# Adding half of the residual in the output: copies placed early, accumulating transfers from POOL, and a new order of the program

## The chip, the cores and the metric

The kernel runs on one core of a Trainium2 chip. The metric is the device time of one execution in microseconds (us), taken as the median of repeated runs; lower is better. The core has five engines with queues of their own: PE (matrix products into PSUM), DVE and ACT (elementwise work), POOL, and SP, which here issues transfers. ACT and POOL can issue transfers too.

## The reference

The input `x` has 2048 tokens of 512 channels. What is computed (helpers as usual, the convolution by FFT in the reference):

```python
xn = layernorm(x)
# A: a long convolution per channel, its kernel from 128 complex states
K  = einsum("dn,dnl,dn->dl", C, exp(dt * A * l), dt * B).real
s  = causal_conv(xn, K) + xn * Dskip
# B: token shift, then an MLP
h  = gelu(layernorm(xn) @ w1)
x1 = xn + concat(shift(h[0], +1), shift(h[1], -1), shift(h[2], +2), shift(h[3], -2)) @ w2
m  = x1 + gelu(layernorm(x1) @ w3) @ w4
return x + s * silu(m)
```

The last line is the one that the change touches: the gated product `s * silu(m)` is added to the residual `x`.

## The kernel before

The tokens lie in SBUF as `X`, 128 partitions by 16 steps by 512 channels (float32). One tile `X` goes through everything: layernorm, the token shift, the MLP's result, the gate, and at last the product.

The program is a list of some 1600 operations that a recorder (`Plan`) collects with their dependencies. A table of numbers, `ORDER`, says in which order they are issued; a letter behind a number (`a` or `v`) says that ACT or DVE takes an operation that either may do. Each engine runs its own operations strictly in that order, and each queue of transfers is issued in it too: an entry that waits holds up what stands behind it. All operations are issued from one helper line, so the profile's rows all name L310, and they are told apart by tiles.

The stages, much interleaved by the order:

- first layernorm, first product (`hT`), token mixing (tiles `x`, `x2h`, `xT`, `w1h`, `ue`, accumulators `pa` and `pb`);
- sixteen chunks of tables for the convolution's kernel (tiles `wv`, `mag`, `eg`, `up`, `EB`, on ACT and DVE), each ending in small products on PE (`pc`, `kev`, `k1e`);
- the MLP in eight groups of 256 tokens, six steps each: `pb` gets `x1T` times `w3h`, ACT and DVE make `ghl` of it, and `pa` sums `ghl` times `w4h`; a group ends with `X<-pa,wsc,X` on DVE. `x1n`, `x1h` and a transposing transfer prepare a group's input;
- the convolution in the frequency domain, in two halves of 256 channels (`hf` 0 and 1), eight steps each (`uin`, `kin`, `kh`, `pr`, `z1e`), whose results go to DRAM (`scr_Zda`, `scr_Zdb`);
- the gate, `X = silu(X)` on ACT, for each of the eight groups of two steps of tokens;
- the end: for each half and group a load `zin` of the result, a product with `is2` into PSUM (`pd` or `pc` in turn, two pairs of banks), and a multiplication into `X` on DVE (`inverse`). After some groups `finish` adds the residual and stores.

The two functions at the end are these (`V` is DVE, `Q` SP, `A` ACT, `T` PE):

```python
    def inverse(hf, g):
        ...
        Q.dma_start(zin, Zd[hf][:, 2 * g : 2 * g + 2].rearrange("p s r d -> p (s r) d"))
        ...
        V.tensor_mul(Xh, Xh, two[k][:, :, :DH])

    def finish(hf, s0, s1):
        ch = slice(hf * DH, hf * DH + DH)
        xr = resid[hf, s0 // 4]
        V.tensor_add(X[:, s0:s1, ch], X[:, s0:s1, ch], xr[:, s0 % 4 : s0 % 4 + s1 - s0])
        by_r(X[:, s0:s1, ch], ov[:, :, s0:s1, ch], store=(Q, A))
```

`X` no longer holds the residual by then, so `keep_tokens` copies the input from DRAM to DRAM (`scr_Rd`, sixteen transfers of 256 KB at any time in the middle of the program), and `residual` loads it back in eight tiles `xr` of 512 KB ahead of `finish`. The copy's only purpose is a layout that loads in long rows. `by_r` stores the two halves of the partitions, one from SP and one from ACT. The second half (`hf` 1) ends with five calls of `finish`, over 4, 4, 4, 2 and 2 steps of tokens.

The order of the groups in the end is 2, 3, 4, 5, 6, 7, 1, 0; group 0 is the last that the MLP makes.

Of the kernel before, what the change touches and what calls it, by code (L numbers as in the profile page):

```python
# [10 lines left out]
F32 = mybir.dt.float32  # L11
# [3 lines left out]
ALU = mybir.AluOpType  # L15
# [4 lines left out]
P = 128  # L20
L = 2048
D = 512
NM = 128
F = 1376
S = 16
# [90 lines left out]
281 188 71a 138v 204 201 358 63 137 356 279 151 282 276 193 152 197a 222 227 157 283 277 228 229 189 65 284 191 64 285
286 519 192 58 149 206 139 148 359 194a 199 230 231 287 66 198 13 288 195 196 232 212 68 207 205 67 520 521 213v 233
236v 360 365 216a 218 69 529 530 76 250 217 156 254a 215 214 251a 237v 289 361 202 74 75a 256 522 290 255 293a 234v
253 524 525 238v 209 31 239 531 235v 77v 252 134 523 260v 269 273a 270a 241v 242 363 210 211 294v 275 272 526 154 532
533 271 307 153 247 534 535 248 208 244 274 243 291v 308a 311a 245 541 135 292v 326 249 240 366 246 261 528 309 310  # L120
537 312 313 330a 160 161 158 538 536 263 266 29 552 553 327v 328 329 339 295v 296 364 159 155 340a 33 554 257v 258 362
539 558 30 379 555 556 264 371 267 259 540 542 543 561 557 559 32 413 414 415 367 268 368 369 544 545 370 262 572 573
12 298a 299 265 578 372 574 34 304 305 331 332 343a 373 560 427 306 301 546a 374 314a 375 376 377 378 391 35 317a 302
547 562 380 381 563 392 393 428 382 418 297 394 318 416 383 344 395 396 384 300 323 342 397 575 548 385 429 315 576
581 324 386 417 577 579 549a 564 565 303 320 321 432 319 398 592 593 399 566a 580 387 567 400 402 550a 341 388 390 401
594 389 316 325 322 598 336 337 333 334 407 404 338 353 352 410 411a 412 433 408a 409 354 335 347 348 583 551 345 430
711 568 569a 405 582 601 349 346 434 420 421 584 570a 437 585 595 597 422 441 709 596 599 435a 438a 439 458 718 612
403 571 586a 436 425 620 600 459a 625 440 442 621 445 613 622 587 443 452 423 460 602 350 446 426 623 624 461 465 614
603 631 419 424 481 444 431 617 447 448 615 449 616 588 589a 590a 450 511a 515a 618 634 619 464 466 451 482a 604 605
626 453 627 478 483 591 606a 645 516a 485 607 472 517 608 351 462a 484 646 512a 513 647 628 463 712 629 630 632 471  # L130
648 650 514 486 649 609a 518 728 721 722 633 491 636 635 479a 723 651 724a 637 480 494 638 473 735 729 654 492a 610a
611 725 493 500 665 666 726 730 731a 639a 732 742a 743a 736 737 640 495a 497 498a 667 668 744 652 727 738a 499 653 750
751 752 739 733 734 715 655 757 758 753a 641 656 746a 747a 748 745 759 642a 496 764 765 657 658 643a 713 674 671 754
501a 670 685 686 687 740 741 755 756 716 853 659a 669 672 749 770 777 778 766a 760a 761 688 689 762 690 771 772 673
763 773a 660 675 661 767 791a 502 676 406 768 691 706 774 779 780a 784 785 769 775 776 644 662a 692 799 819 714 663a
694 820 821 677 693 792a 793 678 786 664 806 800 822 827 828 807 781 823 782 787a 829 824 825 795a 788 796v 852 469
783 679a 797 798 680 681 456 830 831 682a 695 789 790 826 696 697 698 801 813 802a 794 808 1117 467 683a 832 833 699a
809a 454 684 834 803 814 866 700 838 476 804 835 836 805 810 867 841 837 815a 1124 1118 868 477 1119 468 1125 1126 839
811 816 812 1120a 840 455 701 869 702a 703a 704 817 1131 1132 710 1127a 871 842 843 1121 872 886 818 854 844 845 1146
846a 1138a 1139a 870 1122 900 1123 847 848 901 1140 1141 1133 875 1147 849a 850a 1128 1129 1142a 873 855 1130 1134a  # L140
856a 857 888 902 1135 1143a 874 858 1136 1137 1153 1144 1145 851 719 859 1148 1160 860 861 903 905 904 862 1154 863a
877 1155 876 909 864a 906 865 474 878 879 887 1156a 934 880a 881 1166 935 470 936 1149a 1150 707 882 883a 884a 885
# [12 lines left out]
1267a 1261 489 1048 1070 1064 1103 1090 1065 1066a 1262 1067a 1 1072 1268 1272 1073a 1564 1074 1263 1269 1105 1273
1091 1293 1274a 1075 1076 1285a 1077 1078 1294 1079 1080a 1093 1270 1081a 490 1068 1280 1082 1281a 1094 1095 1096
1097a 1275 1276 1404 1286v 1287 1098 1099 1300 1100a 1101a 1104 1295 1106 1107a 1102 1277 1282 1283 1296v 1289a 1108
1288 1297 1109 1111 1110 1301 1284 1403 1405 1112 1290a 1291 1298 1113 1302 1303v 1114v 487 488 1307 507 1292 1406
1407a 1115v 1308 1419 1408 1409 1410 1411 1299 1313 1431 1418 1314 1315 1412 1413 1415a 1327 1417 1414v 1420 1433 1304
1432 1422 1320 1321 1305 1421a 1423 1424 1425 1426 1427 1322 1309v 1328 1445 508 1517 509 1310 1428a 1434 1435a 1429v  # L160
1436 1116 1306 1316a 1565 510 1311 1334v 1437 1342 1438 1447 1439 1440 1441 1343 1525 1416 1317 1442a 1448 1443v 1449a
1518 1446 1450 1312 1329 1323v 1318 1319 1330a 1324 1325 1451 1452 1453 1454 1455 1456a 1461 1457a 1460 1326 1335v
1336 1344 1331 1338a 1459 1462 1463a 1515 1464 1332 1339v 1340 1349 1465 1475 1466 1467 1350 1468 1345a 1536 1469 1526
1473 1356 1430 1470a 1471v 1337 1351 1476 1474 1357 1478 1333 1341 1369 1488 1362 1477a 1479 1480 1481 1482 1483 1487
1363 1364 1444 1484v 1472 1489 1490 1491a 1501 1346 1485v 1492 1352v 1347 1353 1493 1494 1348 1495 1496 1529 1503 1354
1497 1458 1499v 1519 1355 1498a 1504 1505a 1358v 1359 1520 1502 1506 1566 1360 1507 1370 1524 1500 1376 1508 1567 1371
1509 1510 1511 1513a 1486 1365v 1366 1512v 1383 1514 1527 1521 1539 1372v 1373 1530 1528 1537 1377 1361 1367 1368 1531
# [8 lines left out]
class Plan:  # L176
    def __init__(self, nc):
        self.engines = {"PE": nc.tensor, "ACT": nc.scalar, "DVE": nc.vector, "SP": nc.sync}
# [1119 lines left out]
```

## Time and profile before

| what | value |
|---|---|
| median of 3 runs | 513.03 us (512.98 to 513.2) |
| the profiled execution | 512.22 us, its span 510.3 us |
| PE | 488.5 us busy, 96% of the span |
| DVE | 452.9 us busy, 89% |
| ACT | 397.5 us busy, 78%, of it 65.4 us in 51 loads of function tables |
| POOL | 0.7 us busy |
| transfers | 94.26 MB, 185 GB/s over the span |
| granted PE clock | 0.99 |

Busy shares are averages over stages. A busy PE here includes time in which matrix products wait, so the chain of waits and the rows of the timeline say more than the 96%. In a row of the timeline stand the start, the duration, the engine, the operation, and what it writes and reads; brackets give idle time of the engine before it and what ended that.

### The profile page before, as it was taken

How to read it: one execution, taken by the hardware profiler on the slowest of the kernel's cores; microseconds unless marked ns; L12 is line 12 of the kernel's file. 1: busy time of each engine (PE TensorE's matmuls, PEld its weight loads, DVE VectorE, ACT ScalarE, POOL GpSimd, SP SyncE). 2: the span in 40 equal slices, each digit the busy share in tenths (PEclk: the TensorE clock that was granted, in tenths of full speed). 3: DMA queues.
4: the chain of work that ended last, by engine and by line, in shares of the span. 5: the costliest groups of instructions: out<-in, count | busy, mean ns of one | idle time of the engine just before them, and what ended most of it. 6: DMA issues, size and time to landing. Idle time of an engine off the chain costs nothing.

```text
span 510.3 us, 14368 instructions
## 1 busy us (share of the span) xinstructions
PE 488.5 (96%) x6209; PEld 313.1 (61%) x6209; DVE 452.9 (89%) x633; ACT 397.5 (78%) x591; POOL 0.7 (0%) x6
## 2 busy tenths in 40 slices
PE   8788799999999999999999999999999999999993
PEld 8565376585455866767576656656665665756641
DVE  5899999999999999999999999999994687677376
ACT  3999999979969789999999999997864447254330
POOL 0000000000000000000000000000000000000000
PEclk9899999999999999999999999999999999999998
DMA  8997989699253682350768563694579996977987
GB/s 210 237 248 214 278 248 257 180 211 220 75 111 84 135 166 44 64 83 12 155 147 188 144 181 93 146 146 110 145 204 193 282 383 164 306 251 256 317 291 207
DMA packets 157584, 94.26 MB, mean 185 GB/s; under 512 B 98448, under 2 KB 147856, under 8 KB 157136
## 3 DMA queue, kind: packets, MB, share of 16 engines
q1 hardware_dynamic: 155168, 90.98, 69.8%
q10 hardware_dynamic: 2352, 2.36, 1.6%
q8 instruction: 49, 0.80, 0.7%
q14 instruction: 15, 0.12, 0.1%
HBM read 57.14 MB, written 33.55 MB: 178 GB/s over the span
## 4 chain that ended last, share of the span: by engine, by line
PE 61%; DVE 24%; ACT 10%; issue 3%; DMA 1%; POOLq 0%; SPq 0%; POOL 0%; ACTq 0%; DVEq 0%
PE pb L310 23%; PE pa L310 21%; PE pc L310 11%; DVE wv L310 10%; PE pd L310 6%; DVE X L310 3%; ACT wv L310 3%; DVE ghl L310 2%; ACT wst L310 2%; ACT mag L310 1%; DVE up L310 1%; DVE eg L310 1%; ACT ue L310 1%; DVE stats L310 1%; DMA scr_Ud<-ue 1%
## 5 line engine op out<-in xcount | busy, mean ns | idle before, releaser
L310 PE MATMUL pb<-x1T,w3h 128*128 128x256 f16 (+1 forms) x1056 | 125.1, 273 | 0.3 <-issue 0.3
L310 PE MATMUL pa<-w4h,ghl 128*128 128x512 f16 (+1 forms) x528 | 122.5, 380 | 0.0
L310 PEld LDWEIGHTS <-w3h 128*128 128x128 f16 (+1 forms) x1056 | 101.7, 100 | 27.0 <-issue 10.7
L310 PEld LDWEIGHTS <-ghl 128*128 128x128 f16 (+1 forms) x528 | 48.9, 98 | 62.0 <-issue 10.2
L310 ACT ACT_TABLE_LOAD x51 | 65.4, 1283 | 8.9 <-issue 3.7
L310 ACT ACTIVATE wv<-wv 128x2080 f32<-128x2080 int32 x32 | 62.8, 1963 | 0.5 <-DVE wv L310 0.3
L310 ACT ACTIVATE g<-pb,wsc 128x512 f32<-128x512 f32 (+1 forms) x48 | 30.8, 650 | 22.9 <-PE pb L310 18.3
L310 DVE TENSOR_TENSOR wv<-wv,eg 128x2048 f32<-128x2048 f32 x16 | 36.5, 2283 | 1.6 <-ACT wv L310 1.5
L310 DVE TENSOR_TENSOR wv<-mag,wv 128x2048 f32<-128x2048 f32 x16 | 36.5, 2283 | 0.0
L310 DVE SCALAR_TENSOR_TENSOR ghl<-g,wsc,ghl 128x512 f16<-128x512 f32 (+1 forms) x48 | 33.6, 701 | 2.8 <-ACT ghl L310 2.5
L310 PEld LDWEIGHTS pc<-wv 128*32 128x32 f32 x2048 | 29.8, 109 | 6.1 <-issue 3.4
L310 ACT ACTIVATE wv<-wv,halfpi 128x2080 f32<-128x2080 f32 x16 | 32.9, 2055 | 0.1
L310 ACT ACTIVATE mag<-par 128x128 f32<-128x128 f32 x132 | 32.6, 462 | 0.0
L310 PE MATMUL pc<-wv 128*32 128x64 f32 x2048 | 32.4, 220 | 0.0
L310 ACT ACTIVATE ghl<-g,wsc 128x512 f16<-128x512 f32 (+1 forms) x37 | 25.5, 693 | 8.0 <-PE pa L310 7.2
L310 DVE TENSOR_TENSOR pr<-pd,kh 128x1024 f32<-128x1024 f32 x16 | 19.6, 1223 | 13.0 <-ACT kh L310 11.3
L310 PE MATMUL pb<-xT,w1h 128*128 128x256 f16 x240 | 27.6, 273 | 0.0
L310 PE MATMUL pb<-w,hT 128*128 128x512 f32 x58 | 26.6, 599 | 0.0
L310 PEld LDWEIGHTS <-w1h 128*128 128x128 f16 x240 | 22.9, 98 | 5.9 <-issue 3.2
L310 PE MATMUL pa<-w,hT 128*128 128x512 f32 x58 | 26.2, 592 | 0.0
L310 DVE BATCH_NORM_STATS2 stats<-X 128x6 f32<-128x512 f32 x32 | 21.2, 683 | 3.9 <-DMA X<-in_A_u_dram 3.9
L310 PE MATMUL pb<-xT,w 128*128 128x256 f32 x96 | 23.6, 395 | 0.1
(156 smaller groups left out, 809.6 us busy)
## 6 DMA issues: line engine op xcount, KB each, us to landing
wst<-in_B_w_dram SPq DMA_DIRECT2D x20, 512.0 KB, 4.8
scr_Ud<-ue SPq DMA_DIRECT2D x32, 256.0 KB, 3.0
uin<-scr_Ud SPq DMA_DIRECT2D x16, 512.0 KB, 4.9
scr_Kfa<-k1e SPq DMA_DIRECT2D x8, 512.0 KB, 5.3
scr_Rd<-in_A_u_dram SPq DMA_DIRECT2D x16, 256.0 KB, 4.5
cst<-c_gp SPq DMA_DIRECT2D x16, 256.0 KB, 5.4
kin<-scr_Kfa SPq DMA_DIRECT2D x8, 512.0 KB, 4.7
scr_Kfb<-k1e SPq DMA_DIRECT2D x8, 512.0 KB, 6.5
```

The source lines that it names most:

```text
L310: ins = [getattr(self.engines[op.eng], name)(*args, **kw).ins for name, args, kw in op.calls]
```

## The change

For the second half of the channels (`hf` 1) the residual is no longer brought back into SBUF. `keep_tokens` copies that half of the input straight to the output, with as many transfers as before. In the end the product of the gate stays in `X`, and POOL issues transfers that add it onto what lies in the output (`accum_op`). Gone are four loads `xr`, five adds on DVE, and the ten plain stores of that half from SP and ACT; new are ten accumulating transfers on POOL, each behind the copy to its place. `finish` stays as it was for the first half. The whole `ORDER` is new.

```diff
@@ the recorder gets POOL as an engine, tile_mixer_kernel an Engine G for it
+        self.engines = {"PE": nc.tensor, "ACT": nc.scalar, "DVE": nc.vector, "SP": nc.sync, "POOL": nc.gpsimd}
-    Rd = dram.tile([2, P, S, DH], F32, name="scr_Rd")
+    Rd = dram.tile([P, S, DH], F32, name="scr_Rd")
@@ keep_tokens
-                    Q.dma_start(Rd[hf, 64 * r : 64 * r + 64, ss], xv[r, :, ss, hf * DH : hf * DH + DH])
+                    ch = slice(hf * DH, hf * DH + DH)
+                    if hf == 0:
+                        Q.dma_start(Rd[64 * r : 64 * r + 64, ss], xv[r, :, ss, ch])
+                    else:
+                        Q.dma_start(ov[r, :, ss, ch], xv[r, :, ss, ch])
+                        placed[r, k] = plan.ops[-1].idx
@@ new
+    def finish_in_place(s0, s1):
+        ch = slice(DH, D)
+        for r in range(2):
+            G.dma_start(ov[r, :, s0:s1, ch], X[64 * r : 64 * r + 64, s0:s1, ch], accum_op=ALU.add)
+            op = plan.ops[-1]
+            op.deps.add(placed[r, s0 // 4])
+            op.alias.add(placed[r, s0 // 4])
@@ the loop over the end
-        residual(hf, (1, 2) if hf == 0 else (1, 2, 3, 0))
+        if hf == 0:
+            residual(hf, (1, 2))
...
-                finish(hf, *ENDS[hf][k])
+                if hf == 0:
+                    finish(hf, *ENDS[hf][k])
+                else:
+                    finish_in_place(*ENDS[hf][k])
@@ ORDER, 62 lines of numbers: all new, first line
-7 3 8 2 88 5 4 6 89 90 21 91 22 92 93 94 95 79 80 0 96v 81 82 83 84 100a 105 17 85 103 106 86 101 14 104 107 108 87a
...
+2 78 21 31 22 3 0 6 105 106 103 5 104 107 108 109 8 4 79 110 111 80 7 112 17 81 82 83 84 85 86 87v 16 113a 115a 114a
```

The constant that reserves room for POOL's transfers is the same before and after (`dynamic_dma_scratch_size=SCRATCH`, 1024 bytes).

What the new order does at three places. First DVE behind the MLP's last accumulate, where `X<-X,pd` and `X<-X,pc` are multiplications of a group and `X<-X,xr` adds of the residual. Before:

```order
L310 SCALAR_TENSOR_TENSOR X<-pa,wsc,X 128x1024
L310 TENSOR_TENSOR X<-X,pd 128x2x256
L310 TENSOR_TENSOR X<-X,pc 128x2x256
L310 TENSOR_TENSOR X<-X,pd 128x2x256
L310 TENSOR_TENSOR X<-X,xr 128x4x256
L310 TENSOR_TENSOR X<-X,pc 128x2x256
L310 TENSOR_TENSOR X<-X,pd 128x2x256
L310 TENSOR_TENSOR X<-X,xr 128x4x256
```

And after, from the add ahead of the accumulate on:

```order
L309 TENSOR_TENSOR X<-X,xr 128x4x256
L309 SCALAR_TENSOR_TENSOR X<-pa,wsc,X 128x1024
L309 TENSOR_TENSOR X<-X,pd 128x2x256
L309 TENSOR_TENSOR X<-X,pc 128x2x256
L309 TENSOR_TENSOR X<-X,xr 128x4x256
L309 TENSOR_TENSOR X<-X,pd 128x2x256
L309 TENSOR_TENSOR X<-X,pc 128x2x256
```

Before, every second multiplication or so is followed by an add, up to the last instruction; after, one add of the first half is left, and eight bare multiplications end DVE's work, of which two are shown.

Second POOL, whose whole work before is the making of an identity matrix at the start:

```order
L1294 UNCONDITIONAL_BRANCH
masks.py:197 MEMSET ident 128x128
masks.py:199 ISA
masks.py:199 AFFINE_SELECT ident<-ident 128x128
L1294 UNCONDITIONAL_BRANCH
```

After:

```order
masks.py:197 MEMSET ident 128x128
masks.py:199 ISA
masks.py:199 AFFINE_SELECT ident<-ident 128x128
L309 DMA out_dram<-X 64x4x256 x6
L309 DMA out_dram<-X 64x2x256 x4
L1310 UNCONDITIONAL_BRANCH
```

Ten transfers have come, six of 256 KB and four of 128 KB, and nothing else stands between them.

Third SP's queue at the end, with buffer numbers. The loads `zin` of a half are counted 0 to 7 as the end uses them. Before, those of the second half are `zin_529` (0), `zin_530` to `zin_535` (1 to 6, with `zin_534` number 5) and `zin_536` (7):

```order
L310 DMA xr_520<-scr_Rd_58 128x1024
L310 DMA zin_533<-scr_Zdb_62 128x1024
L310 DMA zin_529<-scr_Zdb_62 128x1024
L310 DMA zin_530<-scr_Zdb_62 128x1024
L310 DMA zin_532<-scr_Zdb_62 128x1024
L310 DMA zin_535<-scr_Zdb_62 128x1024
L310 DMA out_0_dram<-X_83 64x4x256
L310 DMA zin_536<-scr_Zdb_62 128x1024
L310 DMA zin_534<-scr_Zdb_62 128x1024
```

After, those of the second half are `zin_525` (0) to `zin_532` (7), so `zin_527` is number 2; `zin_522` and `zin_523` are numbers 5 and 6 of the first half:

```order
L309 DMA zin_523<-scr_Zda_61 128x1024
L309 DMA zin_522<-scr_Zda_61 128x1024
L309 DMA zin_526<-scr_Zdb_62 128x1024
L309 DMA out_0_dram<-X_83 64x4x256
L309 DMA zin_525<-scr_Zdb_62 128x1024
L309 DMA zin_532<-scr_Zdb_62 128x1024
L309 DMA xr_520<-scr_Rd_58 128x1024
L309 DMA xr_517<-scr_Rd_58 128x1024
L309 DMA zin_524<-scr_Zda_61 128x1024
L309 DMA zin_528<-scr_Zdb_62 128x1024
L309 DMA out_0_dram<-X_83 64x4x256
L309 DMA zin_527<-scr_Zdb_62 128x1024
```

Before, the last store that stands ahead of any load of the second half has number 7 and number 5 behind it; after, it has number 2 behind it. Ahead of the loads of the first half's numbers 6 and 5 stand, just above the rows shown, three loads of the second half. Elsewhere 46 operations change between DVE and ACT (22 go to ACT, 24 to DVE), and ACT loads 53 tables instead of 51, among other things since `warm`, an activation of one column that stood at the start, now stands in its last MLP work.

More of the change, by code (lines that the diff above doesn't have):

```diff
@@ L116 @@
[L116 to L130, printed above, removed]
@@ new lines @@
+130 155 225 150a 151 152 359 179v 131 61 188 181a 184v 132 223 180v 219 224 71a 203v 519 221 133 220 185 149 186a 200v
+182 183a 193 148 145 190 222 62 191 57 64 226 711 136a 197a 199 360 201 227 189 63 194a 212 192 280 228 276 278 198
+229 65 277 206 196 230 282 138v 66 68 283 231 279 281 232 134 284 216a 233 285 157 195 235a 357 286 67 287 532 218 520
+217 213a 214 215 529 58 160 250 254a 76 137 69 74 75a 521 236v 209 30 522 202 234v 135 256 251a 269 288 530 255 273a
+161 531 524 525 241v 252 289 253 156 355 523 274 270a 238v 158 365 204 205 207 208 526 210 290 275 356 533 211 139
@@ new lines @@
+257v 237v 272 307 311a 271 308a 239 292v 242 77a 243 240 534 535 244 245 313 309 310 312 291v 260v 258 247 248 249 552
+553 326 246 294v 295v 293v 266 528 554 327v 330v 267 339 29 538 329 328 261 358 537 296 536 340a 331 555 363 541 539
+558 32 262 556 540 364 159 263 264 297 361 413 259 414 542 543 544 557 559 366 545 265 301 362 369 268 415 370 546a
+314a 302 371 372 578 379 332 427 572 573 298a 418 33 574 34 299 428 315 367 368 343a 561 375 380 377 560 381 562 304
+305 376 378 575 382 373 374 303 35 391 392 429 300 393 317a 318 383 320 12 306 323 563 394 395 547 416 384 396 417 385
@@ new lines @@
+688 689 644 690 692 456 819 772 784 785 676 791a 662a 663a 709 675 820 773a 694 786 821 768 779 799 800 677 827 678
+806 693 807 780a 769 781 829 830 823 774 775 822 832 792v 776 795v 782 783 664 824 793 825 679a 680 787a 788 789 695
+828 826 696 833 831 796a 797 708 681 790 801 682a 794 808 802a 813 834 814 697 698 809a 835 837 836 803 804 805 798
+1117 841 699a 810 811 474 866 867 838 812 683a 868 1124 815a 869 1125 1126 839 816 1138a 700 684 707 476 1118 1119
+1120a 701 817 702a 703a 704 854 1131 1132 840 886 872 843 871 842 844 845 846a 477 875 1121 1146 818 870 847 1139a
@@ new lines @@
+505 1176a 1182 968 506 1171 1187a 1188a 920 969 921 1177 942 923 956 720 1189 1172 924a 925 944 926 1202 927 978 976
+928 1195 1196 979 1178 1191v 1203 929 930 1183v 1184 1192v 931a 932a 919 1190 945 972 980 977 1179 946 981 947 973
+948a 1197 970 1193 933 1185 1198a 1186 971 974 949 975 982 983 950 1209 951a 952a 1204 957 1205a 958a 1194 1215 955
+987 959 1015 1210 1016 984 986 985 1199 1222 1200 1201 1211a 1223 960 1206 1224 1017 962 961 963 990 1216 1217 988 989
+964 1035 1207 1212 1018 1021 1208 992 1218a 1219 991 1024 965a 1229 1236a 1237v 953 1230 1231 1213 1214 1244 1251 966a
@@ new lines @@
+1238 967 1225a 1020 1001 993 994 995a 1220 996 997 1252 1019 998a 999a 1049 1050 1226 1240a 1245 1221 1022 1246 1232a
+1002 1051 1003 1004 1037 1005a 1052 1000 1023 1227 1006 1233 1007 1008 1228 1258 1234 1241a 1242 1009 1243 1010 1235
+1247a 1248 1249 1011 1054 1026 1053 1250 1013a 1025 1058 1012a 1239 1014 1027 1028 1055 1056 1253 1264 1029a 1030 1031
+1032a 1265 1083 1084 1085 1033a 1259 1036 714 1038 1057 1271 1254a 715 1255 1039a 1266 1069 1040 1041 1042 1043 1044
+1278 1256 1257 1045 1086 1071 1088 1047a 1279 1059 1060 1092 1046a 1260a 1061 1062 1087 1034 1089 1267v 1048 1103
@@ new lines @@
+1063a 1064 1272 1273 1261 1065 1268 1090 1262 1263 1066a 1091 1067a 1072 1280 1300 1070 1073a 1074 1075 1269 1270
+1281a 1076 710 1077 1293 1078 1079 1093 1094 1294 1105 1080a 1274a 1275 1081a 1285v 1095 1096 1097v 1098 1286v 1068
+1276 1082 1404 487 1104 1099 1100a 488 1287 1277 1101a 1106 1282 1289v 1290v 1291 1283 1102 1301 1107v 1108 1403 1295
+1307 1445 1296v 1297 1109 1110 1288 1111 1405 1284 1112 489 490 1298 1302 1303a 1113 1115v 1299 1308 1309v 1310 1114a
+1406 1407a 1408 1292 1304 1305 1313 1320 1409 1410 1411 1517 1412 1413 1414v 1306 1417 1116 1419 507 1420 1415a 508
@@ new lines @@
+1418 1422 1421a 1423 1526 1311 1424 1425 1426 1321 1322 1536 1416 1433 1314 1459 1315 509 1427 1327 1431 1429a 510
+1334v 1428a 1434 1435a 1432 1323v 1324 1436 1342 1437 1438 1439 1440 1328 1329 1430 1316a 1317 1343 1441 1443a 1442v
+1349 1312 1335a 1336 1446 1447 1448 1461 1449a 1450 1451 1452 1460 1453 1318 1319 1325 1454 1455 1344 1330a 1489 1525
+1338a 1331 1339a 1356 1456v 1462 1475 1457a 1474 1458 1464 1340 1350 1326 1357 1332 1463a 1465 1466 1467 1468 1519
+1469 1337 1351 717 1333 1471a 1473 1470a 1476 1477a 1345v 1346 1478 1341 1369 1362 1363 1479 1480 1481 1482 1444 1483
@@ new lines @@
+1484a 1487 1347 1485a 1524 1490 1491a 1352v 1488 1353 1501 1492 1493 1494 1495 1496 1515 1520 1348 1354 1355 1497
+1499v 1364 1365a 1498a 1502 1503 1376 1504 1358v 1506 1370 1505a 1507 1508 1529 1377 1371 1383 1500 1509 1510 1511
+1521 1472 1359 1360 1513a 1366 1527 1486 1512v 1530 1514 1516 1539 1546 1588 1361 1528 1583 1580 1518 1384 1522 1531
+1385 1367 1368 1540 1555 1378 1372a 1373 1379v 1537 1549 1374 1375 1380 1381 1567 1382 1538 1397 1390 1386v 1387 1
+1532 1533 1541 1542 1564 1593 1398 1547 1548 1545 1550 1535 1391 1558 1392 1393v 1394 1575 1544 1388 1551 1389 1399v
@@ L177, in __init__ @@
     def __init__(self, nc):
-        self.engines = {"PE": nc.tensor, "ACT": nc.scalar, "DVE": nc.vector, "SP": nc.sync}
+        self.engines = {"PE": nc.tensor, "ACT": nc.scalar, "DVE": nc.vector, "SP": nc.sync, "POOL": nc.gpsimd}
         self.ops = []
@@ L421 @@
     plan = Plan(nc)
-    V, A, T, Q = [Engine(plan, e) for e in ("DVE", "ACT", "PE", "SP")]
+    V, A, T, Q, G = [Engine(plan, e) for e in ("DVE", "ACT", "PE", "SP", "POOL")]
     E = Either(plan)
```

70 lines of the change are left out of this document (22 added, 48 removed).

## The prediction

> **What bounds the kernel now.** I read the page first, then the busy time by stretch, the chain of waits, and the timeline of the end. The profiled execution took 512.2 us, 1.9 outside its span, and the median of the three runs is 513.03.
>
> ```profile
> span 510.3 us, 14368 instructions
> PE 61%; DVE 24%; ACT 10%; issue 3%; DMA 1%; POOLq 0%; SPq 0%; POOL 0%; ACTq 0%; DVEq 0%
> ```
>
> ```profile
> core 0: us, PE busy (x) PEld busy (x) DVE busy (x) ACT busy (x) POOL busy (x), PEclk, DMA share, GB/s
> 0.00:50.00 50.00, 41.46 (x225) 32.84 (x227) 42.83 (x121) 40.74 (x74) 0.70 (x6) 0.97 0.93 230
> ...
> 250.00:300.00 50.00, 49.95 (x821) 31.55 (x823) 49.69 (x58) 48.25 (x81) 0.00 (x0) 1.00 0.65 152
> ...
> 350.00:400.00 50.00, 50.00 (x862) 30.32 (x860) 40.58 (x49) 30.77 (x40) 0.00 (x0) 1.00 0.74 170
> 400.00:450.00 50.00, 50.00 (x805) 31.79 (x804) 36.01 (x49) 22.60 (x29) 0.00 (x0) 1.00 0.95 303
> 450.00:511.00 61.00, 51.34 (x448) 28.87 (x446) 37.01 (x48) 19.79 (x23) 0.00 (x0) 0.96 0.79 255
> ```
>
> Up to about 300 us DVE has no gaps (49.69 of 50), from 350 on PE alone is full. POOL does 0.70 us of work in the whole span, all at the start. The chain shows the hand-over and where the end begins:
>
> ```profile
> 264.98 1.16 DVE wv L310
> ...
> 267.54 1.42 PE pb L310 x12
> ...
> 286.14 1.31 PE pb L310 x12
> ...
> 479.79 11.67 PE pa L310 x54
> 491.49 1.29 DVE X L310
> ```
>
> So there are two parts. The body ends when the last `pa` group of the MLP ends, at T = 491.49. Behind it lies an end of 18.8 us, in which DVE, PE and DMA hand ten groups from one to the other:
>
> ```profile
> 491.38 1.08 PE L310 MATMUL pd<-zin,is 128*64 128x256 f32 x8
> 491.49 1.28 DVE L310 SCALAR_TENSOR_TENSOR X<-pa,wsc,X 128x1024 f32<-128x1024 f32 x1 [2.08 <-PE pa L310]
> 492.30 1.03 PE L310 MATMUL pc<-zin,is 128*64 128x256 f32 x8
> 492.81 1.06 ACT L310 ACTIVATE X<-X 128x1024 f32<-128x1024 f32 x1 [0.76 <-DVE X L310]
> 493.90 0.69 DVE L310 TENSOR_TENSOR X<-X,pc 128x512 f32<-128x512 f32 x1 [0.53 <-ACT X L310]
> 495.16 1.22 DVE L310 TENSOR_TENSOR X<-X,xr 128x1024 f32<-128x1024 f32 x1
> 498.62 0.68 DVE L310 TENSOR_TENSOR X<-X,pc 128x512 f32<-128x512 f32 x1
> 499.22 0.68 DVE L310 TENSOR_TENSOR X<-X,pd 128x512 f32<-128x512 f32 x1
> 504.87 0.69 DVE L310 TENSOR_TENSOR X<-X,xr 128x512 f32<-128x512 f32 x1
> ```
>
> The reader is to see that DVE alternates multiplications (0.68, started 0.60 apart when nothing is awaited) with adds of `xr` (1.22 and 0.69), and is done at 505.56, T + 14.1. From there to the end 4.7 us go into the last stores:
>
> ```profile
> L310 SPq DMA_DIRECT2D out_dram<-X x9: 596/607/1110, 469.5 to 505.6; - x9
> L310 ACTq DMA_DIRECT2D out_dram<-X x9: 612/632/1158, 469.5 to 505.6; - x9
> DMA to landing us min/median/max: 3.1/4.3/8.3
> ```
>
> ```profile
> DMA to landing us min/median/max: 3.4/3.5/3.7
> ```
>
> The first three lines are all stores of the output, the last one those issued after 505: they land at 505.6 + 3.7 = 509.3, and 1.0 us more closes the span.
>
> **The change, part by part.**
>
> *The body in its new order.* The kinds and numbers of PE's instructions stay. What can move T is DVE's load ahead of the hand-over. Between DVE and ACT 46 operations change sides; ahead of the tenth table chunk (265 us) ten come to DVE and eight leave it. Prices:
>
> ```profile
> L310 DVE TENSOR_SCALAR X<-X,rs,bs 128x512 f32<-128x512 f32 x11 | 5.9, 539 | 0.0
> L310 DVE TENSOR_SCALAR x<-X,rs 128x512 f32<-128x512 f32 x2 | 0.9, 475 | 0.0
> L310 DVE TENSOR_SCALAR x2h<-X,rs 128x512 f16<-128x512 f32 x5 | 2.3, 481 | 0.0
> L310 DVE COPY ue<-pa 128x1024 f32<-128x1024 f32 x2 | 2.4, 1222 | 0.1
> L310 DVE CAST x1h<-x1n 128x512 f16<-128x512 f32 x6 | 2.5, 425 | 2.0 <-ACT x1n L310 1.6
> L310 DVE COPY z1e<-pd 128x512 f32<-128x512 f32 x6 | 4.1, 684 | 2.8 <-PE pd L310 2.8
> ```
>
> Coming: two `X`, two `x`, two `x2h`, one `ue`, one `x1h`, one `x1n` (as `X`) and one copy of `xT` out of PSUM (as the `z1e` copy): 1.08 + 0.95 + 0.96 + 1.22 + 0.43 + 0.54 + 0.68 = 5.9. Leaving: three `X`, two `x`, one `ue`, one `x1h`, one copy of `par` (as `z1e`): 1.62 + 0.95 + 1.22 + 0.43 + 0.68 = 4.9. Net 1.0 us more on DVE. I take +0.9 for T, since ACT's lighter load gives a little back. Bounds: -1.0 (the start waits on loads anyway, 42.83 of 50, and PE's next table step stands one 1.3-us group earlier) to +2.4 (other DVE work drawn forward of the same chunk as well).
>
> *Table loads.* ACT gets two more:
>
> ```profile
> L310 ACT ACT_TABLE_LOAD x51 | 65.4, 1283 | 8.9 <-issue 3.7 <-DVE ghl L310 2.8 <-PE pb L310 1.6
> ```
>
> Around `warm`, which now stands in ACT's last MLP work, a load of the square root and one back to the gelu take 2 x 1.28. ACT is busy for 19.79 of the last 61 us there, and PE has 7 us of `pa` groups in hand: zero. Without that cover 2.6 us.
>
> *SP's queue.* It loses four `xr` loads and five stores, ACT loses five stores; the sixteen copies stay, eight of them aimed at the output. Loads of `zin` move. Number 5 of the first half refills the slot that number 2 frees; between the two PE has four `pa` groups of 1.30, two `pb` of 1.31 and one zin of 0.92, together 8.7 us.
>
> ```profile
> L310 SPq DMA_DIRECT2D zin<-scr_Zdb x8: 320/626/1284, 470.9 to 490.9; - x8
> DMA to landing us min/median/max: 3.7/7.8/10.1
> ```
>
> Some 0.5 us of issue and 7.8 to landing are 8.3: hidden, by 0.4 us only; at 10.1 it costs 1.9. Number 2 of the second half (`zin_527`) now stands behind a store that waits for DVE's add just ahead of T: issued at about T - 1, used at about T + 5. The last two loads of before, issued just ahead of T, landed so:
>
> ```profile
> L310 SPq DMA_DIRECT2D zin<-scr_Zdb x2: 1161/1222/1284, 489.7 to 490.9; - x2
> DMA to landing us min/median/max: 5.6/5.7/5.8
> ```
>
> At 5.8 it is in time; at 7.8 it is 1.8 late, which POOL's queue (next) would swallow. Zero, bounds 0 to +1.9.
>
> *The end.* Five adds leave DVE, 3 x 1.22 + 2 x 0.69 = 5.0 us. They don't all come off: the multiplications now meet PE's two PSUM pairs. A round of two groups is PE 1.08, DVE 0.68 and two hand-overs (0.03 from the gate's end at 493.87 to 493.90; I take 0.06), thus 1.9. With T' the new end of the body: accumulate 1.28; the gate's table load now waits behind three stores on ACT, so the gate ends at T' + 2.8 (before T + 2.4); multiply 0.7, the remaining add 1.2, then two multiplications: numbers 0 and 1 of the second half are ready at T' + 6.0, the next pairs at 7.9 and 9.8, the last two groups at 10.8 and 11.8. DVE is 2.3 us earlier than before.
>
> In place of adds and stores come ten accumulating transfers on POOL, one behind the other: 3 x 2 of 256 KB, 2 x 2 of 128 KB. The copies that they add to are issued by SP ahead of the last two MLP groups, the last of them some 50 us of PE work before T, against 8.3 for the slowest landing above: that wait costs nothing. No row shows POOL issuing a transfer. Lower bound: the 0.60 us that SP takes for the same store. Upper bound: POOL may start the next only when the last has landed, 4.3. The nearest rows are the same stores' slowest issues in the end, 1.11 and 1.16; I take 1.0. Ten from T' + 6.0 on are a queue that never runs dry: the last starts at T' + 15.0, lands 4.3 later (it reads its destination too, so the median and not the 3.5 of the last store), and 1.0 closes: T' + 20.3, against T + 18.8. That is +1.5.
>
> The Trainium skill's page "DMA: Bandwidth & Descriptors", section "Anatomy of one DMA — SWDGE (gpsimd) path", gives a transfer from POOL about 2.0 us plus its bytes over 436 GB/s, by estimate 2.6 us for 256 KB. With that in place of 4.3 the end would be -0.2 and the total 513.7; here the stores from SP and ACT already take 4.3, so I stay with the row.
>
> *Sum.* 0.9 + 0 + 0 + 1.5 = +2.4 us: 514.6 for the profiled execution, 515.4 for the median.
>
> **Rivals.**
>
> *POOL is as quick as SP (faster).* At 0.60 each no queue forms: the last pair is issued at T' + 12.4 and 13.0, lands after 3.7, closes at T' + 17.7: -1.1. With the body at zero 511.9. It decides below 0.72 us per issue with T' unmoved (6.0 + 9 x 0.72 + 5.3 = 17.8). For it: SP's row. Against: two queues did the stores before, one does them now.
>
> *POOL may hold only a few open.* The kernel reserves 1024 bytes (SCRATCH) for such transfers. With three open, the fourth waits for the first to land: starts at T' + 6.0, 7.0, 8.1, 10.3, 11.3, 12.4, 14.6, 15.6, 16.7, 18.9, and with 4.3 and 1.0 the end is T' + 24.2: +5.4, 519.3 in all. One at a time: 6.0 + 43 + 1.0, +31, 544. Nothing in the trace speaks for or against it. The Trainium skill says on the same page, "DMA: Bandwidth & Descriptors", in its sections "SWDGE vs HWDGE vs iDMA" and "Terms", that these descriptors of 16 bytes lie in rings in SBUF: by estimate 64 places, of which a transfer of 256 rows over 16 engines takes 17, so three fit. No run here shows it.
>
> *It cancels.* DVE's 2.3 us earlier pay for POOL's issues (0.85 us each gives T' + 18.9), and the body moves by under 1: 513.
>
> **How the numbers follow.** About 0.2% (1.0 us) is what a measurement can tell from no change. Queue on POOL, as summed: 0.50, at 514 to 518.5. Quick POOL: 0.18, 511.9. Cancels: 0.15. Few open: 0.14 for three, 0.03 for one. Slower is 0.48 + 0.17 = 0.65, faster 0.18, same 0.17. The range goes from 511.0 (quick, with a body of -0.9) to 521 (three open with the body at +2.4), and leaves out one at a time and the tails of both ends.
>
> **What would show it.** Right: DVE's last instruction some 12 us behind the last `pa`; POOL rows of about 1 us each, without idle time between them, to the end; the span ending about 20 us behind T'. Wrong: gaps on POOL released by a DMA (few open); gaps released by DVE X (quick); PE waiting for a `zin` load; or T' away from 492.4 by more than 2 us, which would make the new order, not the transfers, the cause.

## The result, and the profile after

The changed kernel takes 536.15 us (median of 4 runs, 535.67 to 536.29) against 513.0 of the kernel before on the same chip: ratio 1.0448, 95% interval 1.0432 to 1.0464. It is 23 us slower. The direction was predicted, the size was not (+2.4).

From here on M is the start of DVE's last accumulate (`X<-pa,wsc,X`), which follows the last `pa` by 0.03 us. M divides the program in two: before, 491.49 us of body and an end of 18.8; after, 493.76 of body and an end of 40.7. So 2.3 us came in the body and 21.9 in the end.

First the page of the changed kernel: its span, the busy times, POOL's queue (packets, MB, share of 16 engines' span) and the shares of the chain.

```profile
span 534.5 us, 14337 instructions
...
PE 491.2 (92%) x6209; PEld 315.6 (59%) x6209; DVE 449.6 (84%) x630; ACT 397.1 (74%) x591; POOL 11.0 (2%) x16
...
q0 software_dynamic: 2208, 2.10, 3.4%
...
PE 71%; ACT 7%; DVE 7%; DMA 6%; issue 5%; POOL 2%; SPq 1%; POOLq 0%; ACTq 0%; DVEq 0%
```

POOL is busy for 11 us of 534. The table by stretch shows where it stands alone:

```profile
core 0: us, PE busy (x) PEld busy (x) DVE busy (x) ACT busy (x) POOL busy (x), PEclk, DMA share, GB/s
350.00:400.00 50.00, 49.25 (x921) 30.78 (x919) 45.47 (x53) 26.28 (x35) 0.00 (x0) 1.00 0.80 187
400.00:450.00 50.00, 49.03 (x798) 31.38 (x798) 33.51 (x45) 25.80 (x33) 0.00 (x0) 1.00 0.91 274
450.00:511.00 61.00, 53.45 (x520) 30.17 (x512) 33.44 (x45) 24.60 (x28) 3.25 (x3) 0.98 0.72 230
511.00:535.00 24.00, 0.00 (x0) 0.00 (x0) 0.00 (x0) 0.00 (x0) 7.01 (x7) 0.50 0.57 66
```

In the last 24 us every compute engine is at zero, and POOL itself is busy for only 7.01 of them. The two stretches from 350 to 450, which were 50.00 of 50 on PE before, now have 1.7 us of gaps. The timeline of the end, first DVE and then all of POOL:

```profile
493.76 1.28 DVE L309 SCALAR_TENSOR_TENSOR X<-pa,wsc,X 128x1024 f32<-128x1024 f32 x1 [1.33 <-PE pa L309]
...
500.49 0.69 DVE L309 TENSOR_TENSOR X<-X,pd 128x512 f32<-128x512 f32 x1 [1.18 <-PE pd L309]
...
505.10 0.69 DVE L309 TENSOR_TENSOR X<-X,pc 128x512 f32<-128x512 f32 x1 [0.17 <-PE pc L309]
```

```profile
499.92 1.19 POOL L309 DMA_DIRECT2D out_dram<-X  x1 [498.62 <-DMA out_dram<-X]
504.88 1.04 POOL L309 DMA_DIRECT2D out_dram<-X  x1 [3.76 <-issue]
509.48 1.02 POOL L309 DMA_DIRECT2D out_dram<-X  x1 [3.56 <-issue]
513.92 1.04 POOL L309 DMA_DIRECT2D out_dram<-X  x1 [3.42 <-issue]
518.52 1.02 POOL L309 DMA_DIRECT2D out_dram<-X  x1 [3.56 <-issue]
523.14 2.03 POOL L309 DMA_DIRECT2D out_dram<-X  x2 [3.60 <-issue]
527.72 2.93 POOL L309 DMA_DIRECT2D out_dram<-X  x3 [2.55 <-issue]
```

DVE is done at 505.79, 12.0 behind M, and from then on all data lie ready. Yet POOL starts a 256-KB transfer only every 4.6 us: 1.03 us of issue, then some 3.5 us of idle time "<-issue", which means that the profile shows no semaphore that ended it. The sixth 256-KB transfer and the first of 128 KB go back to back, and so do the last three of 128 KB. The time from a POOL issue to its landing in this kernel:

```profile
DMA to landing us min/median/max: 3.1/4.3/4.8
```

A start every 4.6 us and a landing of 4.3 say: the next starts when the one before has landed. Taken one by one from the trace, the six starts behind idle time stand 0.25 to 0.32 us behind the landing of an earlier transfer (the second at 504.88, the first having landed at 504.62). Something holds one 256-KB transfer at a time, but lets smaller ones overlap.

### The profile page after: what moved, and what is told of

Read it like the earlier page. It is cut to its first block, busy times and chain, and to the rows that moved or that the text cites. A ratio compares the mean times of both kernels' runs of the same rounds, so it can differ in the third digit from the quotient of the medians.

```text
span 534.5 us, 14337 instructions
## 1 busy us (share of the span) xinstructions
PE 491.2 (92%) x6209; PEld 315.6 (59%) x6209; DVE 449.6 (84%) x630; ACT 397.1 (74%) x591; POOL 11.0 (2%) x16
## 3 DMA queue, kind: packets, MB, share of 16 engines
q0 software_dynamic: 2208, 2.10, 3.4%
## 4 chain that ended last, share of the span: by engine, by line
PE 71%; ACT 7%; DVE 7%; DMA 6%; issue 5%; POOL 2%; SPq 1%; POOLq 0%; ACTq 0%; DVEq 0%
PE pb L309 30%; PE pa L309 22%; PE pc L309 13%; PE pd L309 6%; DVE wv L309 3%; POOL out_dram L309 2%; DMA uin<-scr_Ud 1%; ACT ue L309 1%; ACT mag L309 1%; DMA xr<-scr_Rd 1%; SPq L309 1%; ACT wv L309 1%; DMA out_dram<-X 1%; DMA X<-in_A_u_dram 1%; DMA x1T<-x1h 1%
```

## The experiments

Theory A: the room for POOL's transfers (SCRATCH, 1024 bytes) is cut into places of 16 bytes, 64 per DMA engine, and an added row takes two of them. (The 16 bytes and the 64 are the estimate of the prediction; the runs vary the room in bytes and don't show the size of a place.) Theory B: transfers that add are serial, whatever the room. Beside these stands the question how much the new order contributes. Ratios are against the kernel before on the same chip (medians 512.7 to 513.0), with 95% intervals; M and the end come from the profiled execution, which lies up to 1.8 us from the median (`plain`).

| kernel | median us | ratio | M | end |
|---|---|---|---|---|
| before | 513.0 | 1 | 491.5 | 18.8 |
| changed kernel | 536.15 | 1.0448 (1.0432-1.0464) | 493.8 | 40.7 |
| ring_1088 | 522.86 | 1.0191 (1.0175-1.0206) | 492.9 | 27.9 |
| ring_2048 | 520.10 | 1.0139 (1.0120-1.0158) | 493.8 | 25.4 |
| ring_4096 | 559.95 | body altered | 534.5 | 24.2 |
| plain | 515.08 | 1.0042 (1.0021-1.0063) | 494.0 | 20.7 |
| halves | 525.72 | 1.0247 (1.0220-1.0275) | 495.3 | 30.2 |
| old_order | 536.78 | 1.0456 (1.0430-1.0482) | 492.8 | 42.8 |
| new_order_adds | 517.82 | 1.0092 (1.0074-1.0109) | 494.6 | 20.5 |
| first_only | 514.35 | 1.0028 (1.0015-1.0041) | 492.4 | 20.2 |
| first_two | 515.13 | 1.0036 (1.0021-1.0052) | 493.2 | 20.5 |
| two_open4 | 514.63 | 1.0034 (1.0021-1.0047) | 491.4 | 20.3 |
| two_banks | 515.52 | 1.0046 (1.0034-1.0059) | 492.0 | 21.7 |
| before_banks | 512.61 | 0.9994 (0.9985-1.0003) | 492.2 | 18.2 |

### Sixty-four bytes more

```diff
-SCRATCH = 1024
+SCRATCH = 1088
@@ to make the room, also in the next kernel
-    ident = keep([P, P], "ident")
+    ident = at(107008, [P, P], F32, "ident")
-    ones = keep([1, P], "ones")
+    ones = at(107520, [1, P], F32, "ones")
```

> The changed kernel with 1088 bytes reserved for POOL's transfers in place of 1024, nothing else. In the changed kernel POOL starts its 256-KB transfers one at a time, 4.6 us apart, with 3.4 to 3.8 us of idle time between them that no semaphore ends. Theory A, places: the reserve is cut into descriptors of 16 bytes, 64 places per DMA engine of which 63 can be used; a row that is added needs two of them, so a 256-KB transfer of 256 rows takes 33 places on each of 16 engines, two are 66, and one at a time fits. 1088 bytes are 68 places, 67 to be used: two fit. POOL's rows should then come in pairs, the next pair when the first of the last pair has landed (some 4.5 us behind its start), and the end should shrink from 40.8 to about 28 us behind the last pa: 523 to 525 us. Theory B, adding is serial: a transfer that adds must have landed before the next starts, whatever room there is; the time stays at 536 with the same idle times.

Measured: 522.86 us, 13.3 less, and an end of 27.9. POOL's first rows:

```profile
499.08 2.23 POOL L309 DMA_DIRECT2D out_dram<-X  x2 [497.78 <-DMA out_dram<-X]
504.00 1.03 POOL L309 DMA_DIRECT2D out_dram<-X  x1 [2.69 <-DVE X L309]
505.70 1.02 POOL L309 DMA_DIRECT2D out_dram<-X  x1 [0.67 <-issue]
508.40 1.03 POOL L309 DMA_DIRECT2D out_dram<-X  x1 [1.67 <-issue]
```

The first two now start back to back, and the third follows 4.9 us behind the first, when that has landed. Sixty-four bytes more, four places by theory A, let a second transfer in. Theory B falls: nothing else in the end was changed.

### 2048 bytes

```diff
-SCRATCH = 1024
+SCRATCH = 2048
```

> The changed kernel with 2048 bytes reserved for POOL's transfers; to make the room, the tiles ident and ones lie at another address, nothing else. Theory A: 127 usable places, three transfers of 33 at once and a fourth of 17. POOL's ten rows of 1.0 us should run with one or two short gaps, the end about 22 us behind the last pa, 516 to 519 us. Theory B: 536 with unchanged gaps.

Measured: 520.10 us, an end of 25.4; a little slower than expected. POOL's first four transfers,

```profile
500.01 2.24 POOL L309 DMA_DIRECT2D out_dram<-X  x2 [498.70 <-DMA out_dram<-X]
502.74 1.01 POOL L309 DMA_DIRECT2D out_dram<-X  x1 [0.49 <-DVE X L309]
504.66 1.04 POOL L309 DMA_DIRECT2D out_dram<-X  x1 [0.91 <-issue]
```

and the time from POOL's issues to their landing:

```profile
DMA to landing us min/median/max: 4.4/5.4/6.4
```

Three start as the data come, the fourth waits for a landing. But the landing is now 5.4 us in the median instead of 4.3, so something beside the places grows when more are open.

### 4096 bytes: the queue that never runs dry

```diff
-SCRATCH = 1024
+SCRATCH = 4096
-    wtile = Ring(area(4 * K2), K2, 4)
+    wtile = Ring(area(3 * K2), K2, 3)
```

> The changed kernel with 4096 bytes reserved for POOL's transfers. To make the room the tile ring wtile has three buffers in place of four, and entries of the order that this forbids are moved behind what they now wait for, so that the body is longer; only the end, counted from the last pa, is to be read. With 2048 bytes the end is still 25.4 us against the 20.3 of the prediction's queue that never runs dry. Theory A: 255 places, seven transfers of 33 open, POOL's ten rows have no gap that only places explain, and the end is the sum of T' + 6.2 to the first start, ten issues of 1.05 to 1.25 and a last landing of 4.3 to 5.4 and the close: 21 to 24 us. Rival: landings grow with the number open (5.4 us with three), and the end stays at 25.

Measured: an end of 24.2 us. All of POOL,

```profile
540.64 2.25 POOL L309 DMA_DIRECT2D out_dram<-X  x2 [539.34 <-DMA zin<-scr_Zdb]
543.58 8.10 POOL L309 DMA_DIRECT2D out_dram<-X  x8 [0.69 <-DVE X L309]
```

and its landings:

```profile
DMA to landing us min/median/max: 4.6/7.6/8.6
```

Eight issues without a gap, 1.01 us each: the premise of the prediction, made true. The last one starts at about 550.7, 16.2 behind M (the prediction had 15.0 behind T'). But it lands at 557.4 by the trace, 6.8 us later and not 4.3. The landings in the line above are counted from the start of a record, and the records of issues back to back overlap, so they hold up to 1.9 us of POOL's own work. Counted from the end of the issue, a 256-KB addition lands in 3.1 to 3.5 us in the changed kernel and in 3.4 to 6.4 here: the growth is real, if smaller. Both expectations hold in part: no place is waited for, and landings grow, so that from 2048 to 4096 bytes the end falls by only 1.2 us.

### Stores in place of additions

```diff
-            G.dma_start(ov[r, :, s0:s1, ch], X[64 * r : 64 * r + 64, s0:s1, ch], accum_op=ALU.add)
+            G.dma_start(ov[r, :, s0:s1, ch], X[64 * r : 64 * r + 64, s0:s1, ch])
```

> The changed kernel with POOL's ten transfers as plain stores (the residual of the second half is left out of the result), 1024 bytes reserved as in the changed kernel. Theory A in its form for added rows: a plain row takes one place, 17 for 256 KB, three are open at once; starts at about 6, 7, 8, 11, 12, 13 us behind the last pa and then one per us: 516 to 518 us. Theory A', any transfer from POOL takes 33 places, added or not: one at a time as now, 534 to 536 us. Theory B: no gaps at all, 515 to 517 us, so A and B differ here only by a gap behind the third row.

This kernel leaves out the residual of the second half. Measured: 515.08 us, with ten runs from 512.78 to 517.50; the profile is of one of 516.86. POOL's queue on the page, POOL in the timeline, and its landings:

```profile
q0 software_dynamic: 672, 2.10, 1.6%
```

```profile
500.23 1.37 POOL L309 DMA_DIRECT2D out_dram<-X  x2 [498.92 <-DMA out_dram<-X]
504.10 1.24 POOL L309 DMA_DIRECT2D out_dram<-X  x2 [2.50 <-DVE X L309]
507.08 3.08 POOL L309 DMA_DIRECT2D out_dram<-X  x5 [1.74 <-issue]
510.35 0.59 POOL L309 DMA_DIRECT2D out_dram<-X  x1 [0.19 <-issue]
```

```profile
DMA to landing us min/median/max: 3.0/3.7/4.0
```

Without `accum_op` POOL issues in 0.62 us, the landing is 3.7, and the gaps of 3.5 us are gone. The second transfer starts right behind the first, so two of 256 KB fit where one addition did (theory A' falls): the transfers of the changed kernel wait because they add. The fifth waits for DVE's product, which ends at 506.43; it starts 0.65 us behind it, as the first does behind its own.

One gap is left that the data don't explain, the 0.19 us before the last row, whose product ended at 508.30. By the trace the fifth transfer landed at 510.03, and the last starts 0.32 behind that, as the additions do behind a landing. This is what 17 places for 256 KB and 9 for 128 KB give: with the fifth still open, the last two of 256 KB and four of 128 KB would be 70, and without it they are 53. So the expectation's 17 places fit this run (on a single gap of 0.19), and its time was too long since plain issues and landings are shorter than it took. The packets of the profile don't count places: the same 2.10 MB go in 672 packets instead of 2208. What adding costs the DMA engines: 3.4% of 534.5 us is 18.2 us of all sixteen engines' time, 1.6% of 514.7 is 8.2.

### The same bytes in smaller transfers

```diff
-            G.dma_start(ov[r, :, s0:s1, ch], X[64 * r : 64 * r + 64, s0:s1, ch], accum_op=ALU.add)
+            for t in range(s0, s1, 2):
+                G.dma_start(ov[r, :, t : t + 2, ch], X[64 * r : 64 * r + 64, t : t + 2, ch], accum_op=ALU.add)
```

> The changed kernel with each accumulating 256-KB transfer cut into two of 128 KB (two steps of tokens each; sixteen transfers in all), 1024 bytes reserved as in the changed kernel. Theory A: 17 places each, three open at once, the next three when the first has landed: three starts per 4.6 to 4.8 us, the last start about 30 us behind the last pa, 529 to 532 us, although POOL issues six transfers more. Theory B, adding is serial whatever the size: sixteen times at least 4.2 us, 565 to 575 us.

Measured: 525.72 us, 10.4 less than the changed kernel although POOL issues six transfers more. Its first seven starts, and its landings:

```profile
500.85 3.10 POOL L310 DMA_DIRECT2D out_dram<-X  x3 [499.55 <-DMA out_dram<-X]
505.65 2.94 POOL L310 DMA_DIRECT2D out_dram<-X  x3 [1.71 <-issue]
509.21 0.95 POOL L310 DMA_DIRECT2D out_dram<-X  x1 [0.62 <-issue]
```

```profile
DMA to landing us min/median/max: 3.3/3.5/4.9
```

Three go back to back, then the first has to land: three of 128 KB fit where one of 256 KB did. It is quicker than expected because a 128-KB addition lands in 3.5 us, not in the 4.2 that I had taken from the changed kernel. (Those 4.2 are the median of four, three of which were issued back to back; the one at 527.72, which was not, landed in 3.1.)

### The order apart from the transfers

```diff
@@ old_order: the changed kernel with the order of before; where the add of a group
@@ stood, its two accumulating transfers
@@ new_order_adds: the kernel before with the new order, its adds and stores where the
@@ transfers stand, the loads xr of the second half behind the last copy, and
-    Rd = dram.tile([2, P, S, DH], F32, name="scr_Rd")
+    Rd = [dram.tile([P, S, DH], F32, name=f"scr_Rd{h}") for h in "ab"]
```

> The changed kernel with the order of the kernel before: each first-half operation, load and product stands where it stood, the two accumulating transfers of a group stand where its add stood, the four loads xr of the second half and the adds and stores are gone. If the transfers are the whole cause, the last pa ends at 491.5 as before, the end is as long as in the changed kernel (40.8 us), and the time is 533 to 535 us: the new order's part is 2.3 us at most. If the new order makes POOL start late or wait, it comes back to about 515 to 520 us.

> The kernel before in the new order: the second half keeps its loads xr, adds and plain stores (the adds and stores stand where the accumulating transfers stand in the new order, the loads xr directly behind the last copy that they read); the copy scr_Rd is split into two tiles by half so that the first half's loads need not wait for the second half's copies. Theory O, the new order itself is slower: the last pa ends at 493 to 494 as in the changed kernel, and with DVE's adds back in the end the time is 514 to 516 us. Theory N, the order alone is neutral and the body's +2.3 comes from the copies to the output or from the missing loads: 512 to 513.5 us.

Measured: the changed kernel in the old order takes 536.78 us, so that the new order isn't what makes it slow. That is about 2 us more than expected: its first addition lands in 6.7 us (4.7 in the changed kernel), and the second waits for it. The kernel before in the new order takes 517.82, 5 us more than before and more than either theory said. PE in the stretches from 350 to 450, first `old_order`, then `new_order_adds`:

```profile
350.00:400.00 50.00, 50.00 (x893) 30.70 (x890) 41.28 (x48) 30.78 (x41) 0.00 (x0) 1.00 0.73 164
400.00:450.00 50.00, 49.95 (x808) 31.80 (x796) 35.41 (x48) 22.73 (x29) 0.00 (x0) 1.00 0.91 286
```

```profile
350.00:400.00 50.00, 49.04 (x935) 30.94 (x942) 45.51 (x54) 25.95 (x34) 0.00 (x0) 1.00 0.79 188
400.00:450.00 50.00, 48.08 (x782) 31.23 (x774) 33.32 (x44) 25.57 (x32) 0.00 (x0) 1.00 0.95 281
```

The old order keeps PE full there with the change as without it; the new one leaves gaps with the change (1.7 us) and without it (2.9). In the changed kernel the two largest stand before products with `kin`:

```profile
400.27 1.10 PE L309 MATMUL pc<-kin,cst 64*32 64x256 f32 x32 [1.00 <-ACT z1e L309]
417.52 1.10 PE L309 MATMUL pc<-kin,cst 64*32 64x256 f32 x32 [0.44 <-issue]
```

Over all profiles M is 491.4 to 493.2 in the seven kernels in the old order (mean 492.2) and 492.9 to 495.3 in the six in the new order (mean 494.1; `ring_4096` apart). The new order costs about 1.9 us of body. In the changed kernel the gaps from 350 to 450 don't account for it. Here is PE up to M, in the changed kernel and then in the kernel before:

```profile
0.00:493.76 493.76, 481.51 (x6131) 310.46 (x6133) 440.51 (x619) 395.38 (x590) 0.70 (x6) 0.99 0.71 178
0.00:491.49 491.49, 478.69 (x6131) 308.03 (x6133) 439.48 (x617) 395.92 (x590) 0.70 (x6) 1.00 0.72 184
```

All gaps of PE together are 12.3 us in the changed kernel and 12.8 before, since the first 100 us have 2.3 less. The same products took 2.8 us longer instead. A part of that may be the execution: in the first 50 us the granted clock was 0.93, against 0.97 in the profile of before (`before_banks`, with the body of before and 0.93, has M at 492.2). In `new_order_adds` the gaps up to M are 14.4 us. Where the new order loses the rest isn't shown.

The 5 us of that kernel are 3.1 of body and 1.7 of end. In the end PE waits for the load of `zin` that stands behind a store,

```profile
500.41 1.08 PE L310 MATMUL pd<-zin,is 128*64 128x256 f32 x8 [1.59 <-DMA zin<-scr_Zdb]
```

and DVE is done 15.7 behind M, where the kernel before had 14.1. (The places of its loads `xr` were my choice, so a part of it may be theirs.)

### Fewer additions: does a mixture beat both?

```diff
@@ first_only: one group of the second half by POOL (k 1 alone), old order, 1024 bytes
@@ first_two: two groups, 2048 bytes
-                    if hf == 0:
+                    if hf == 0 or k not in (1, 3):
                         finish(hf, *ENDS[hf][k])
@@ two_open4: as first_two
-SCRATCH = 2048
+SCRATCH = 2176
@@ two_banks: as two_open4, and before_banks: the kernel before; in inverse
-        k = 2 + turn["pp"] % 2
+        k = 2 + turn["pp"] % 2 if hf == 0 else (1, 0, 3, 2)[(turn["pp"] - 1) % 4]
```

> The kernel before, in its own order, with only the first group of the second half (two transfers of 256 KB) added in the output by POOL; the other four groups keep loads, adds and stores; 1024 bytes reserved. DVE loses one add of 1.22 us out of a stretch without gaps. If POOL's two transfers, 4.6 us apart by the places, stay hidden (they land about 16 us behind the last pa against an end of 18.8), the time falls by 0.8 to 1.2 us against the kernel before: ratio 0.998. If PE's two pairs of banks or a late load zin take the gain, it stays within 0.3 us; if POOL's transfers slow the others' stores, it is slower.

> As the kernel with one group added by POOL, but the first two groups (four transfers of 256 KB) and 2048 bytes reserved (three of 33 places open, as theory A counts). DVE loses two adds, 2.4 us, of which PE's banks give back some. POOL's fourth transfer starts some 11 us behind the last pa and lands 5.4 later, about 17.2 with the close, against 18.8: 1.2 to 2.0 us faster than before, ratio 0.996 to 0.998. If the transfers from POOL with their landing of 5.4 us end last, no change.

> The kernel with the first two groups of the second half added by POOL, in the order of before, now with 2176 bytes reserved (135 usable places, four transfers of 33 as theory A counts) in place of 2048 (127, three); two pairs of small tiles lie elsewhere, nothing else. With 2048 bytes the fourth transfer started 12.3 us behind the last pa with 2.9 us of idle time before it, and the end was 20.6 us. Theory A: all four start without a gap, the last at about 9.6, and land by 16; DVE's last store then ends at about 17.9: 0.9 us faster than before, ratio 0.998. If the gap stays, places are not what holds the fourth.

> As the kernel with two groups added by POOL and 2176 bytes, with the products of the second half spread over four pairs of PSUM banks (pb, pa, pd, pc in turn) in place of two; the MLP no longer needs pa and pb by then. DVE's waits for PE in the end (0.59, 0.17, 0.32 us) should go, DVE be done about 12.2 us behind the last pa, and the end be 16.9 us against 18.8 before: ratio 0.996, 511 us. If PE waits for the last loads zin instead, no gain over two pairs.

> The kernel before with four pairs of PSUM banks for the products of the second half, nothing else. DVE has no gap there between its multiplications and adds, so that the end is DVE's: within 0.3 us of the kernel before. If it is faster by itself, a gain of the kernel with two groups and four pairs is not POOL's.

Measured: 514.35, 515.13, 514.63 and 515.52 us, all four slower than before by 0.3 to 0.5%; all four expectations of a gain were misses. `before_banks` is the same as before within the noise, as expected. What POOL does in `first_two` and then in `two_open4`:

```profile
499.27 3.28 POOL L310 DMA_DIRECT2D out_dram<-X  x3 [497.97 <-DVE X L310]
505.44 1.04 POOL L310 DMA_DIRECT2D out_dram<-X  x1 [2.89 <-issue]
```

```profile
497.52 4.32 POOL L310 DMA_DIRECT2D out_dram<-X  x4 [496.21 <-DVE X L310]
```

With 127 places a fourth transfer waits for the first to land, with 135 it does not: theory A's count once more. DVE is early as well, done 13.2 behind M in `two_open4` and 11.7 in `two_banks`, against 14.1. What takes it back is the landing of the last plain stores of SP and ACT, here with KB and median us to landing, in before, `two_open4` and `two_banks`:

```profile
out_dram<-X SPq DMA_DIRECT2D x2, 128.0 KB, 3.7
out_dram<-X ACTq DMA_DIRECT2D x2, 128.0 KB, 4.0
```

```profile
out_dram<-X SPq DMA_DIRECT2D x2, 128.0 KB, 6.0
out_dram<-X ACTq DMA_DIRECT2D x2, 128.0 KB, 6.2
```

```profile
out_dram<-X POOLq DMA_DIRECT2D x4, 256.0 KB, 8.4
...
out_dram<-X SPq DMA_DIRECT2D x2, 128.0 KB, 8.8
out_dram<-X ACTq DMA_DIRECT2D x2, 128.0 KB, 9.0
```

The reading is that the earlier DVE is, the more stores and additions are under way together, and the longer each takes; no run varies the one without the other. Plain stores count in it as well as additions: in `first_only` just one addition is open at a time, and its two land in 6.1 and 6.5 us. The second of them, held by the places until 505.24, lands at 511.37, and the last store, from ACT, at 511.70; before, the last store landed at 509.27. No version that I ran beats the kernel before by more than the noise.

## Why the prediction was wrong

**The step that failed** is "a queue that never runs dry". The last of the ten issues was to start 15.0 us behind T'; it started 35.9 behind M, since POOL stood idle for a landing before six of them. With it failed the rival "POOL may hold only a few open", which named the cause and was priced wrong: 0.14 for three, 0.03 for one. The estimate behind it counted a place for each row, 17 for 256 KB, so three fitted into 64. The runs put the number at 32 or 33 if one place stays unused: two don't fit into 63 but fit into 67, four don't fit into 127 but fit into 135. (If none stays unused it is 33 or 34; in bytes, which need no size of a place, 256 KB took more than 508 and at most 544 of the room.) That is two places for a row, where `plain` fits one.

The Trainium skill says what this looks like: "Collectives: The Full Stack", in the section "The bandwidth ceiling: the fold count and why AG ≠ RS ≠ AR", states that an addition in the DMA engines needs two source reads, so that it emits two read descriptors per chunk where a copy emits one, and both go on the same ring. The page speaks of another path of transfers; here the counts of places (32 to 34 for an addition, 17 for a store by the one gap of `plain`) and the engines' time (18.2 against 8.2 us for the same bytes) agree with it. I had looked only at the page on DMA, and had treated an addition like a store.

**The size.** The end grew by 21.9 us. Of these the prediction had 1.5. The end of `ring_4096`, 24.2, has no waiting for places: 40.7 - 24.2 = 16.5 us are the places (its body was altered, so this is near and not exact). The other 24.2 - 20.3 = 3.9 are a last start 1.2 us later (data, and issues a little over 1.0), a last landing 2.5 us longer, and a close of 1.3 instead of 1.0. Landings grow with what is under way (median 4.3 us with one addition open, 5.4 with three, 7.6 with up to seven, this last with some of POOL's queue in it); the prediction had taken the landing of 4.3 as fixed. The rival's own number for one at a time, +31, was too high since it took ten landings of 4.3 in a row; the four small transfers overlap.

**Term by term.** POOL's issue, taken as 1.0: 1.04 in the median, right, and the rival "quick POOL" at 0.60 is what a plain store takes (0.62). The first transfer at T' + 6.0: 499.92, T' + 6.2. DVE done at T' + 11.8: 12.0. Both are near by some luck: the product that the first transfer needs ended at T' + 5.6, and POOL started 0.6 behind it (the profile names the landing of a store as what it waited for, which no run tests); DVE's early product and its later wait for PE cancel. The landing of one transfer alone, 4.3: 4.3 in the median, the lowest that 256-KB additions had in any of these kernels. The Trainium skill's fit on "DMA: Bandwidth & Descriptors" ("Anatomy of one DMA — SWDGE (gpsimd) path") gives an estimate of 2.6; the plain stores from POOL, at 3.7, lie above it too.

**The body**, +0.9 predicted, was +2.3 in the two profiles and is about 1.9 over all of them: inside the bounds (-1.0 to +2.4), but the mechanism isn't shown, so the bounds held by luck. The term came from DVE's 1.0 us more of work. In the kernels of the new order DVE has 7 to 11% of the chain, against 24% before, but it has 4% in `first_only` too, whose order is the old one and whose M is 492.4, so the chain doesn't decide. PE's gaps behind 350, where I had not looked at the loads, are made up for by fewer gaps in the first 100 us.

**`zin` number 2** of the second half: late, as priced at 0 to +1.9. It landed 6.1 us behind its issue, at 499.24, and PE's product with it starts 0.13 later; DVE stood idle for 1.18 us there, of which PE's product is a part. POOL's queue swallowed it as the text said; it is bare in `new_order_adds`. The table loads cost nothing that the end's rows show.

**What would show it** worked: "gaps on POOL released by a DMA" was the sign of few open. The gaps came with "issue" as their releaser: the wait was for room, as SCRATCH shows, and the profile names no semaphore for it.

## What to carry to other kernels

A transfer that adds is not a store with a free addition: before moving an add from an engine into transfers, count two places per row against the room reserved for them, and let the timeline show whether POOL's issues stand back to back. If they stand a landing apart with no semaphore named, more room or smaller transfers help at once (64 bytes gave 13 us here). And in the tail of a kernel, time saved on an engine is only worth what the transfers behind it can land: `two_open4` and `two_banks` had DVE done 0.9 and 2.4 us earlier, and lost more in stores that took 6 to 9 us instead of 4.

## What the runs showed of the hardware that I had not expected

- A 256-KB addition of 256 rows of 1 KB takes more than 512 and at most 544 bytes of the room reserved for POOL's transfers, or more than 508 and at most 540 if 16 of the room stay unused; in places of 16 bytes that is 32 to 34. The packets in the profile (2208 for ten transfers on sixteen engines, so 17 for 256 KB on each) show only half of that.
- POOL issues a plain store in 0.59 to 0.63 us (the first of the kernel in 0.75) and, when no other issue of it runs, an addition in 0.95 to 1.04 (the first in 1.13 to 1.19), almost the same for 128 and 256 KB.
- The same 2.10 MB took 672 packets as stores and 2208 as additions, and 8.2 against 18.2 us of the engines' time.
- An addition of 256 KB lands in 4.1 to 4.7 us with no other addition open in the changed kernel, and in 6.1 and 6.5 in `first_only`, beside plain stores. In `two_banks`, with four additions open beside stores, one took 11.9, and a 128-KB store from SP 8.8 in the median, against 3.7 in the kernel before.
